# Operations charged by their measured steps, and two weight stages moved into attention

## The chip, the cores and the metric

The kernel runs on one core of one Trainium2 chip. The metric is the device time of one execution in microseconds (us), lower is better. A core has five engines with queues of their own: PE (matmul; PEld is its weight load), DVE (vector), ACT (scalar), POOL and SP, of which POOL and SP issue nearly all DMAs here. Each engine works its queue strictly in order, and engines wait for each other by semaphores.

## The reference

Three layers follow each other, all in float32. `q`, `k`, `v` are [4, 12, 448, 64]; `x` of the second layer is [1792, 768].

```python
scores = scale * np.matmul(q, k.transpose(0, 1, 3, 2)) - np.log(S)
attn = np.matmul(1.0 / (1.0 + np.exp(-scores)), v)            # sigmoid, no softmax
x = attn.transpose(0, 2, 1, 3).reshape(1792, 768)
h = np.maximum(np.maximum(x @ w1, x @ w2), x @ w3) @ moe_w_out   # weights 768 x 768
h = h @ w_in                                                  # 768 x 2048
g = np.maximum(h, 0.0) + alpha * np.minimum(h, 0.0)
out = g @ w_out                                               # 2048 x 768
```

## The kernel before

**Products.** Every matrix product after attention is a 2 x 2 block product with seven multiplications in place of eight (Strassen and Winograd): an index `k` from 0 to 6 names the multiplication, sums of blocks stand on either side. Each float32 operand is split into a high and a low word ("h" and "l"), and three matmuls (l by h, h by l, h by h) make one product of full precision. A step `(u, k, g)` is 9 matmuls of 128 x 128 by 128 x 448 for unit `u`, multiplication `k`, token half `g`; a unit has 14 steps. Units 0 to 8 are the first product (three column blocks for each of `w1`, `w2`, `w3`; the maximum is taken on DVE as units arrive), then units 100 to 105 the product with `moe_w_out` (`third` in the code, its left operands made first of all, in attention, and stored in DRAM), then units 9 to 16 the product with `w_in`; the product with the last `w_out` follows in 42 groups of 24 matmuls (`e_group`).

**Words.** The weights arrive as 64-bit floats, half a block at a time (128 x 384, tile `wr`, four buffers), and `word_ops` makes float32 of them with integer operations: two on ACT (L240, L243) and three on DVE (L250, L251, L259). With `early=True` the first of the ACT ones goes to DVE instead (L247). `unit_ops` takes four halves, makes four sums (L289), and cuts seven operands `f_0` to `f_6` into high (L278, on ACT, or on DVE for `moe_w_out`) and low word (L282, DVE). These are the left sides of a unit's steps. `words_out` makes four more halves per unit for the last product and stores them to DRAM. The pool `ws` holds words and cut operands in 21 buffers; a cut `f_k` of unit `u` may be made once step `(u-1, k, 1)` stands in the program, which frees its two buffers.

**Who sets the order.** PE's order is written out by hand. The rest is filled in by a planner: `op` puts an operation with an engine letter ("A", "D", "Q" for a DMA) and a price in columns into a list; after each step of PE `advance` gives ACT and DVE credit (`STEP`, two thirds of it for ACT) and `emit`s whatever is ready while its engine's credit is above zero. A price is the operation's columns plus 150. What PE needs and has not been emitted yet is forced out by `need`. Evictions of a step's result (ACT copies at L852 and L867, DVE sums and maxima at L289) are emitted right behind the step and charged by `spend`.

**Around the change.** In attention (12 units of 7 chunks) `load_half` brings in the first four weight halves during unit 1, the `moe_w_out` operands are planned at `(u, c) == (1, 0)`, those of unit 0 at `(4, 0)`. At the first step of unit `u`, `begin` plans the operands of unit `u + 1`. `h_store` forms sums of the finished maxima after every third unit and stores them; `held` names the ones that must be out before the next unit writes there, and `evict` forces all of them at its first eviction.

Of the kernel before, what the change touches and what calls it, by code (L numbers as in the profile page):

```python
# [62 lines left out]
def kernel(  # L63
# [11 lines left out]
    B, H, S, D = BATCH, HEADS, SEQ, P // 2  # L75
# [7 lines left out]
    HF = HK * P  # L83
# [42 lines left out]
    halves, zc, zu, zo = half_blocks()  # L126
# [13 lines left out]

    class Op:
        def __init__(self, engine, cols, fn, deps, gate, lag):
            self.engine, self.cols, self.fn, self.deps, self.gate = engine, cols + 150, fn, deps, gate
            self.step, self.ends, self.after = None, [], []

            self.lag = lag
# [1 line left out]

    free = {"wr": 8, "wl": 4, "wk": 8, "ws": 5, "wf": 4, "rr": 14, "e": 4, "a": 7}
    urgent, flow = [], []
    STEP = 1700
    credit = {"A": 0, "D": 0}

    def op(engine, cols, fn, *deps, gate=None, soon=False, lag=0):
# [41 lines left out]
                    n += 1  # L198

    def spend(engine, cols):  # L200
        credit[engine] -= cols + 150

    maker = {}

# [26 lines left out]
    def word_ops(z, gate=None, early=False):  # L231


        st = {}

        def first():
            st["r"] = wraw.pop(z)
            st["T"] = wslot(f"wt{z}", U32)
            if not early:
                nc.scalar.activation(  # L240
                    st["T"].bitcast(F32), st["r"][:, :, 1].bitcast(F32), AF.Abs, scale=2.0**-112
                )
            nc.scalar.activation(st["r"][:, :, 0], st["r"][:, :, 0], AF.Copy, scale=2.0**-29)  # L243

        def whole():
            if early:
                nc.vector.tensor_scalar(  # L247
                    st["T"].bitcast(F32), st["r"][:, :, 1].bitcast(F32), 2.0**-112, None, ALU.mult
                )
            nc.vector.tensor_scalar(st["T"], st["T"], 3, None, ALU.logical_shift_left)  # L250
            nc.vector.scalar_tensor_tensor(  # L251
                out=st["r"][:, :, 0],
                in0=st["r"][:, :, 1],
                scalar=0x80000000,
                in1=st["r"][:, :, 0],
                op0=ALU.bitwise_and,
                op1=ALU.bitwise_or,
            )
            nc.vector.tensor_tensor(out=st["T"], in0=st["r"][:, :, 0], in1=st["T"], op=ALU.add)  # L259
            word[z] = st["T"].bitcast(F32)  # L260
            if z >= 20:
                load_half(z + 4)

        o = op(
            "A", (1 if early else 2) * HF, first,
            gate=lambda: z in since and tick[0] > since[z] + 3 and (gate is None or gate()),
        )
        o = op("D", (4 if early else 3) * HF, whole, o)
        if z < 20:

            op("Q", 0, lambda: load_half(z + 4), o, lag=1)
        return o

    def split_ops(dst, make, src, w, *deps, engine="A", **kw):

        def hi():
            dst[0] = make("h")
            (nc.scalar.copy if engine == "A" else nc.vector.tensor_copy)(dst[0], src())  # L278

        def lo():  # L280
            dst[1] = make("l")
            nc.vector.tensor_sub(dst[1], src(), dst[0].bitcast(F32))  # L282

        o = op("D", w, lo, op(engine, w, hi, *deps, **kw), soon=kw.get("soon", False))
        maker[id(dst)] = o
        return o

# [4 lines left out]

    cd = {}
    pending = [0]

    def words_via(z):

# [14 lines left out]

        return back

    def unit_ops(u, z, gates=None, words=word_ops, store=False, more=[]):

        f = [{} for _ in range(7)]
        t = {}
# [20 lines left out]
        def cut(k, src, *deps):  # L339
            def make(x):  # L340
                if store and x == "h":
                    pending[0] += 1
                return wslot(f"f{u}_{k}{x}", F32R)

            o = split_ops(f[k], make, src, HF, *deps, gate=gates[k], engine="D" if store else "A")
            cuts.append(o)
            if store:
                cd[u, k] = [dpool.tile([P, HF], F32, tag=f"c{u}{k}{x}", name=f"cd{u}_{k}{x}") for x in "hl"]

                def put():  # L350
# [151 lines left out]
    def attention(apool, ps_s, ps_v):  # L502
# [118 lines left out]
        for u in range(nu):  # L621
            for c in range(NK):
                scores(u, c)
                if c == 0 and u:
                    for m in (NK - 2, NK - 1):
                        av(u - 1, m)
                    close(u - 1)
                elif c > 1:
                    av(u, c - 2)
                    if u == 0 and c in (4, 5):  # L630
                        to_x(0, 0, (5 - c,))
                if u == 1 and 1 <= c <= 4:
                    load_half(c - 1)
                if (u, c) == (1, 0):
                    for r in range(HK):
                        done += unit_ops(-1 - r, zc[r], words=lambda z: word_ops(z, early=True), store=True)
                if (u, c) == (2, 2):
                    nc.sync.dma_start(out=alpha_sb, in_=alpha)
                if (u, c) == (4, 0):
                    free_ws = lambda: all(o.step is not None for o in done)  # L640
                    unit_ops(0, zu[0], words=lambda z: word_ops(z, gate=free_ws))
                if u and c == 1:
                    load_v(u + 1, nc.gpsimd)
                if u and c < 4:
                    load(u + 1, "kq"[c % 2], c // 2)
                if c == 0:
                    advance(1800, 800)
                elif c != 1:
                    advance(1400, 450)
# [31 lines left out]
    def ff(ps_m, swap, turn_left):  # L681
# [4 lines left out]
        L = ND0 - 1  # L686
# [72 lines left out]
        def h_store(u, g):  # L759
# [14 lines left out]
                b["T"] = slot(f"h{g}{r}_t", "c")  # L774
                tensor_op(b["T"], B12, B11, ALU.subtract)

            put(0, lambda: B11)
            o21, o22 = put(1, lambda: B21), put(6, lambda: B22)
            o1 = op("D", TW, t1, soon=True)
            p1 = put(2, lambda: b["T"], o1)  # L780
            o3 = op("D", TW, lambda: tensor_op(B12, B22, B12, ALU.subtract), o1, soon=True)
            put(4, lambda: B12, o3)
            o2 = op("D", TW, lambda: tensor_op(b["T"], B22, b["T"], ALU.subtract), p1, soon=True)
            put(3, lambda: b["T"], o2)
            o4 = op("D", TW, lambda: tensor_op(B21, B21, b["T"], ALU.subtract), o2, o21, soon=True)
            held[g] = [o22, put(5, lambda: B21, o4)]

        def evict(u, g, i, t, src, other=None):

# [18 lines left out]
            j = u % 3  # L808
            key = (i, 2 * g + t)
            if j == 0:  # L810
                if g in held:
                    need_ops(*held.pop(g))
                cur[key] = slot(f"mx{u}_{i}_{key[1]}", "c")
            if other is not None:
                dst = other if j else cur[key]
# [147 lines left out]
        def begin(u):  # L963
# [2 lines left out]
            elif u == ND0:  # L966
                pass
            elif u != L:
                last[:] = unit_ops(u + 1, zu[u + 1])
                if u < NU - 3:  # L970
                    words_out(u)
                elif u < L:
# [7 lines left out]
                    for r in range(HK - 1):  # L980
                        reload(0, c, r, lambda: (L, 0, 0) in made)

        via, last = [], []
        began, run = set(), []
        inner = (0, 2, 3, 1, 4, 6, 5)
        third = [(0, 0)]
# [403 lines left out]
```

## Time and profile before

| | |
|---|---|
| device time, median of 3 runs | 928.92 us (928.04 to 932.2) |
| profiled execution, its own time | 928.69 us |
| its span, first to last instruction | 926.8 us |
| PE, DVE, ACT, POOL busy | 94%, 71%, 57%, 16% of the span |
| mean granted PE clock | 0.983 |

All durations are from the profiled execution, and places are us from the start of its span. Attention lasts to 132.9, the first product to 412.6, that with `moe_w_out` to 500.5, that with `w_in` to 719.4, the last to 923.4. PE's busy time is modelled, so that the number of its matmuls in a stretch tells more than the share.

### The profile page before, as it was taken

To read this page: it belongs to the slowest core of one execution; us is meant where nothing else is said; L and a number is where in the kernel's file an instruction comes from. 1 tells how busy PE (TensorE), PEld (TensorE's weight loads), DVE (VectorE), ACT (ScalarE), POOL (GpSimd) and SP (SyncE) were. 2 spreads that over 40 slices of the span, in tenths; PEclk is the share of its full clock that TensorE was granted. 3 is DMA by queue.
4 is the path that set the end of the run, shared out by engine and by line. 5 is a ranking of instruction groups with operands and counts; after the bars stand their busy time and mean duration, and the time that the engine had idled before them with its cause. 6 is when DMAs were issued, how large, how long until landed. Compare 5 with 4: busy or idle time off the path is not lost.

```text
span 926.8 us, 14153 instructions
## 1 busy us (share of the span) xinstructions
PE 869.6 (94%) x4878; PEld 765.1 (83%) x4878; DVE 654.3 (71%) x1289; ACT 527.8 (57%) x1021; POOL 148.5 (16%) x276
## 2 busy tenths in 40 slices
PE   9999997698889989887999899989999999999998
PEld 4478985687778878776999799978999999999997
DVE  1767766477778878765767788887876958777741
ACT  6888975345355445454546667667666735444520
POOL 2454000001300131331000013321221100000110
PEclk9999999899999999999999999999999999999999
DMA  7899510245644665688663146643445889644411
GB/s 240 286 333 340 166 54 0 70 135 149 221 145 136 183 212 170 204 302 277 205 194 103 40 154 213 232 168 129 168 168 177 304 306 392 238 144 149 151 51 50
DMA packets 77607, 170.45 MB, mean 184 GB/s; under 512 B 11120, under 2 KB 51856, under 8 KB 77536
## 3 DMA queue, kind: packets, MB, share of 16 engines
q1 hardware_dynamic: 59472, 104.81, 36.6%
q0 software_dynamic: 17776, 64.41, 18.9%
q8 instruction: 38, 0.62, 0.3%
q10 hardware_dynamic: 288, 0.34, 0.1%
q14 instruction: 33, 0.27, 0.1%
HBM read 123.12 MB, written 46.40 MB: 183 GB/s over the span
## 4 chain that ended last, share of the span: by engine, by line
PE 85%; DVE 11%; issue 2%; ACT 2%; DMA 0%; POOL 0%; DVEq 0%; ACTq 0%; POOLq 0%
PE u_0X L672 15%; PE u_1X L672 13%; PE eW L672 9%; PE eX L672 9%; PE u_0W L672 7%; PE sc L543 7%; PE pav L564 7%; PE u_1W L672 7%; PE u_0V L672 4%; PE u_1V L672 3%; PE eV L672 3%; DVE mx L289 2%; DVE wr L251 1%; DVE u L289 1%; DVE wt L259 1%
## 5 line engine op out<-in xcount | busy, mean ns | idle before, releaser
L543 PE MATMUL sc<-qt,kt 64*64 64x448 f32 x672 | 108.2, 541 | 0.1
L564 PE MATMUL pav<-a,vt 64*64 64x448 f32 x672 | 106.8, 537 | 0.0
L551 ACT ACTIVATE a<-sc,bias_s 128x896 f32<-128x896 f32 x84 | 83.3, 1008 | 15.2 <-PE sc L543 14.1
L543 PEld LDWEIGHTS sc<-qt,kt 64*64 64x64 f32 x672 | 55.7, 134 | 21.0 <-issue 12.9
L259 DVE CUSTOM_DVE_ANT_0 wt<-wr,wt 128x768 uint16<-128x768 uint16 x112 | 62.6, 559 | 3.9
L564 PEld LDWEIGHTS pav<-a,vt 64*64 64x64 f32 x672 | 54.0, 132 | 13.6 <-issue 7.8
L251 DVE SCALAR_TENSOR_TENSOR wr<-wr 128x384 uint32<-128x384 uint32 x112 | 61.9, 553 | 3.7 <-ACT wr L243 3.1
L243 ACT ACTIVATE wr<-wr 128x384 uint32<-128x384 uint32 x112 | 61.5, 550 | 1.4 <-DVE f-1_3h L278 0.7
L867 ACT COPY u<-u_0X 128x448 f32<-128x448 f32 x40 | 21.3, 534 | 66.7 <-PE u_0X L672 66.7
L240 ACT ACTIVATE wt<-wr 128x384 f32<-128x384 f32 x100 | 55.2, 552 | 0.4 <-DMA wr<-in_weights_dram 0.4
L752 POOL DMA_DIRECT2D gd<-r x48 | 26.1, 544 | 163.0 <-DVE r L719 150.9
L719 DVE SCALAR_TENSOR_TENSOR r<-n,nalpha,r 128x448 f32<-128x448 f32 x64 | 42.9, 682 | 11.3 <-ACT n L716 10.8
L938 POOL DMA_DIRECT2D wd<-wt x32 | 17.4, 544 | 197.6 <-DVE wt L259 186.8
L289 DVE TENSOR_TENSOR u<-u_0W,u 128x448 f32<-128x448 f32 x34 | 21.2, 623 | 35.7 <-ACT u L867 31.5
L289 DVE TENSOR_TENSOR u<-u_1W,u 128x448 f32<-128x448 f32 x34 | 21.2, 623 | 31.5 <-ACT u L867 20.6
L250 DVE TENSOR_SCALAR wt<-wt 128x384 uint32<-128x384 uint32 x112 | 40.1, 358 | 3.5 <-ACT wt L240 3.0
L867 ACT COPY u<-u_1X 128x448 f32<-128x448 f32 x40 | 21.4, 534 | 32.8 <-PE u_1X L672 32.8
L579 DVE COPY x<-pav 128x448 f32<-128x448 f32 x12 | 7.5, 625 | 33.7 <-PE pav L564 33.7
L672 PE MATMUL u_0W<-x_2h,f_2l 128*128 128x448 f32 x27 | 12.2, 453 | 19.6 <-DVE f_2l L282 19.6
L852 ACT COPY u_0V<-u_0X 128x448 f32<-128x448 f32 x20 | 10.3, 517 | 31.8 <-PE u_0X L672 31.8
L1264 ACT COPY p<-eW 128x448 f32<-128x448 f32 x12 | 6.4, 533 | 32.9 <-PE eW L672 32.9
L672 PEld LDWEIGHTS u_0W<-x_2h,f_2l 128*128 128x128 f32 x27 | 5.9, 217 | 23.0 <-DVE f_2l L282 22.6
(814 smaller groups left out, 2832.4 us busy)
## 6 DMA issues: line engine op xcount, KB each, us to landing
wr<-in_weights_dram SPq DMA_DIRECT2D x96, 384.0 KB, 3.5
gl<-gd SPq DMA_DIRECT2D x79, 224.0 KB, 4.3
wl<-wd SPq DMA_DIRECT2D x64, 192.0 KB, 4.5
gd<-r POOLq DMA_DIRECT2D x48, 224.0 KB, 2.8
gl_T<-gdT SPq DMA_DIRECT2D x32, 224.0 KB, 5.1
hr<-hd POOLq DMA_DIRECT2D x28, 224.0 KB, 5.3
wr<-in_weights_dram POOLq DMA_DIRECT2D x16, 384.0 KB, 6.0
wd<-wt POOLq DMA_DIRECT2D x32, 192.0 KB, 3.8
```

Of the source, the lines that this page charges most:

```text
L240: nc.scalar.activation(st["T"].bitcast(F32), st["r"][:, :, 1].bitcast(F32), AF.Abs, scale=2.0**-112)
L243: nc.scalar.activation(st["r"][:, :, 0], st["r"][:, :, 0], AF.Copy, scale=2.0**-29)
L250: nc.vector.tensor_scalar(st["T"], st["T"], 3, None, ALU.logical_shift_left)
L251: nc.vector.scalar_tensor_tensor(out=st["r"][:, :, 0], in0=st["r"][:, :, 1], scalar=0x80000000, in1=st["r"][:, :, 0], op0=ALU.bitwise_and, ...
L259: nc.vector.tensor_tensor(out=st["T"], in0=st["r"][:, :, 0], in1=st["T"], op=ALU.add)
L289: nc.vector.tensor_tensor(out=out, in0=a, in1=b, op=op)
L543: nc.tensor.matmul(sc[g * KH : (g + 1) * KH, j, :S], keys[u, z][r, m * KH : (m + 1) * KH], queries[u, z][r], start=True, stop=True,)
L551: nc.scalar.activation(a, sc[:, :, :S], AF.Sigmoid, bias=bias_s, scale=scale)
L564: nc.tensor.matmul(pv[key][j * D : (j + 1) * D, :S], vts[u][r, m, j], a[r, j], start=start, stop=stop,)
L672: nc.tensor.matmul(ps[:, : rh.shape[-1]], lt, rh, start=(start and z == 0), stop=(stop and z == len(mms) - 1), skip_group_check=True,)
L719: nc.vector.scalar_tensor_tensor(out=s["r"], in0=s["n"], scalar=nalpha[:, f : f + 1], in1=s["r"], op0=ALU.mult, op1=ALU.add,)
L867: nc.scalar.copy(side[u, g, k], banks[X][:, :TW])
```

## The change

Prices come closer to the distance at which operations follow each other: 100 columns on top for ACT and 90 for DVE in place of 150, a high word cut on DVE at half its columns, 100 more for the whole-word operation, and `STEP` is 1760 in place of 1700. The first weight halves are loaded during attention's unit 0, the `moe_w_out` operands are planned at `(0, 4)` in place of `(1, 0)`. Unit 0's words are made the early way and its high words cut on DVE. Unit 1 is planned at attention's unit 9; so `begin` of unit 0 plans nothing, and each later `begin` the next unit as before. `held` becomes four lists, forced one at each of the four evictions.

```diff
+    EXTRA = {"A": 100, "D": 90, "L": 0, "Q": 0}
-            self.engine, self.cols, ... = engine, cols + 150, ...
+            self.engine, self.cols, ... = engine, cols + EXTRA[engine], ...
-    STEP = 1700
+    STEP = 1760
-        o = op("D", (4 if early else 3) * HF, whole, o)
+        o = op("D", (4 if early else 3) * HF + 100, whole, o)
-        o = op("D", w, lo, op(engine, w, hi, *deps, **kw), soon=kw.get("soon", False))
+        o = op("D", w, lo, op(engine, w if engine == "A" else w // 2, hi, *deps, **kw), soon=...)
-    def unit_ops(u, z, gates=None, words=word_ops, store=False, more=[]):
+    def unit_ops(u, z, gates=None, words=word_ops, store=False, engine="A"):
-            o = split_ops(f[k], make, src, HF, *deps, gate=gates[k], engine="D" if store else "A")
+            o = split_ops(f[k], make, src, HF, *deps, gate=gates[k], engine=engine)
...
-                if u == 1 and 1 <= c <= 4:
-                    load_half(c - 1)
-                if (u, c) == (1, 0):
+                if u == 0 and c > 2:
+                    load_half(c - 3)
+                if (u, c) == (0, 4):
                     for r in range(HK):
-                        done += unit_ops(-1 - r, zc[r], words=lambda z: word_ops(z, early=True), store=True)
+                        done += unit_ops(..., words=lambda z: word_ops(z, early=True), store=True, engine="D")
...
-                    unit_ops(0, zu[0], words=lambda z: word_ops(z, gate=free_ws))
+                    unit_ops(0, zu[0], words=lambda z: word_ops(z, gate=free_ws, early=True), engine="D")
+                if (u, c) == (9, 0):
+                    last[:] = unit_ops(1, zu[1], words=lambda z: word_ops(z, early=True))
...
-            held[g] = [o22, put(5, lambda: B21, o4)]
+            held[g] = [[p0], [p4], [o22, o2, o3], [p3, put(5, lambda: B21, o4)]]
-                if g in held:
-                    need_ops(*held.pop(g))
+                if held.get(g):
+                    need_ops(*held[g].pop(0))
...
-                last[:] = unit_ops(u + 1, zu[u + 1])
+                if u:
+                    last[:] = unit_ops(u + 1, zu[u + 1])
```

PE's order is the same in both kernels, instruction by instruction. DVE's changes throughout. Before, around the low word `f6_2l`, which unit 6 needs at its fifth step (`u5` and `mx` are evictions, `h01_t` and `h11_t` sums of `h_store`, `wt` words):

```order
L251 SCALAR_TENSOR_TENSOR wr58_3184<-wr58_3184 128x384
L259 ISA wt58_3259<-wr58_3184,wt58_3259 128x768
L289 TENSOR_TENSOR mx3_0_3_2774<-mx3_1_3_2696,mx3_0_3_2774 128x448
L289 TENSOR_TENSOR h01_t_3297<-mx3_1_1_2679,h01_t_3297 128x448
L289 TENSOR_TENSOR mx3_1_0_2717<-mx3_1_0_2717,h01_t_3297 128x448
L250 TENSOR_SCALAR wt59_3277<-wt59_3277 128x384
L251 SCALAR_TENSOR_TENSOR wr59_3207<-wr59_3207 128x384
L259 ISA wt59_3277<-wr59_3207,wt59_3277 128x768
L289 TENSOR_TENSOR h11_t_3342<-mx3_1_3_2696,h11_t_3342 128x448
L289 TENSOR_TENSOR mx3_1_2_2735<-mx3_1_2_2735,h11_t_3342 128x448
L289 TENSOR_TENSOR wu6_3412<-wt58_3259,wt59_3277 128x384
L282 TENSOR_TENSOR f6_2l_3416<-wu6_3412,f6_2h_3414 128x384
L289 TENSOR_TENSOR wt58_3259<-wt56_3186,wt58_3259 128x384
```
It stands behind unit 5's last maximum (`mx3_0_3`, from step `(5, 6, 1)`) and behind the sums of `h_store`. After, the same operation:

```order
L252 TENSOR_SCALAR wt60_3228<-wt60_3228 128x384
L253 SCALAR_TENSOR_TENSOR wr60_3155<-wr60_3155 128x384
L261 ISA wt60_3228<-wr60_3155,wt60_3228 128x768
L284 TENSOR_TENSOR f6_2l_3267<-wu6_3226,f6_2h_3245 128x384
L291 TENSOR_TENSOR wt56_3134<-wu6_3226,wt56_3134 128x384
L252 TENSOR_SCALAR wt61_3231<-wt61_3231 128x384
L253 SCALAR_TENSOR_TENSOR wr61_3160<-wr61_3160 128x384
L261 ISA wt61_3231<-wr61_3160,wt61_3231 128x768
L291 TENSOR_TENSOR u5_0_4_3286<-u5_0W_3199,u5_0_4_3286 128x448
L291 TENSOR_TENSOR mx3_1_1_2765<-u5_0_4_3286,mx3_1_1_2765 128x448
L291 TENSOR_TENSOR wt57_3137<-wt57_3137,wt56_3134 128x384
```
It now stands ahead of `u5_0_4`, the eviction of step `(5, 4, 0)`, ten steps of PE before the step that reads it.

DVE at the start of the `moe_w_out` product, before (`h0_00l` and its like are the low words of the reloaded maxima, read by that product's first steps; `u8_1_4` is evicted after step `(8, 4, 1)`, the step before):

```order
L282 TENSOR_TENSOR h0_1l_4135<-mx6_1_0_3542,h0_1h_4118 128x448
L289 TENSOR_TENSOR mx6_0_1_3581<-mx6_1_1_3502,mx6_0_1_3581 128x448
L289 TENSOR_TENSOR u8_1_4_4151<-u8_1W_3991,u8_1_4_4151 128x448
L289 TENSOR_TENSOR mx6_1_3_3524<-u8_1_4_4151,mx6_1_3_3524 128x448
L282 TENSOR_TENSOR h0_00l_4159<-hr0_00_3898,h0_00h_3987 128x448
L282 TENSOR_TENSOR h0_01l_4161<-hr0_01_3900,h0_01h_3989 128x448
L282 TENSOR_TENSOR h0_2l_4175<-h0_t_4120,h0_2h_4137 128x448
```
After, where `u8_0_4` is the eviction of step `(8, 4, 0)` and `u7_1_3` belongs to the unit before:

```order
L291 TENSOR_TENSOR u7_1_3_3829<-u7_1W_3780,u7_1_3_3829 128x448
L291 TENSOR_TENSOR mx6_0_3_3676<-u7_1_3_3829,mx6_0_3_3676 128x448
L284 TENSOR_TENSOR f8_5l_3935<-wt75_3746,f8_5h_3904 128x384
L284 TENSOR_TENSOR f8_6l_3951<-wt73_3701,f8_6h_3937 128x384
L284 TENSOR_TENSOR h0_00l_4050<-hr0_00_3965,h0_00h_4030 128x448
L284 TENSOR_TENSOR h0_01l_4052<-hr0_01_3967,h0_01h_4032 128x448
L284 TENSOR_TENSOR h0_20l_4054<-hr0_20_3969,h0_20h_4034 128x448
L291 TENSOR_TENSOR mx6_0_0_3456<-u8_0V_3949,mx6_0_0_3456 128x448
L284 TENSOR_TENSOR h0_21l_4074<-hr0_21_3971,h0_21h_4056 128x448
L284 TENSOR_TENSOR h0_30l_4076<-hr0_30_3989,h0_30h_4058 128x448
L284 TENSOR_TENSOR h0_31l_4078<-hr0_31_3991,h0_31h_4060 128x448
L291 TENSOR_TENSOR u8_0_4_4093<-u8_0W_4001,u8_0_4_4093 128x448
```
The low words for multiplications 0, 2 and 3 moved ahead of unit 8's middle.

POOL's queue at the start, before (`vt` are value blocks for attention, `wr` weight halves; `vt2` waits for a buffer that unit 0 frees):

```order
L532 DMA vt0_99<-in_v_dram 64x512
L532 DMA vt1_116<-in_v_dram 128x896
L137 DMA wr0_268<-in_weights_dram 128x768
L532 DMA vt2_270<-in_v_dram 128x896
L137 DMA wr1_287<-in_weights_dram 128x768
L137 DMA wr2_304<-in_weights_dram 128x768
L137 DMA wr3_321<-in_weights_dram 128x768
```
After:

```order
L535 DMA vt0_99<-in_v_dram 64x512
L535 DMA vt1_116<-in_v_dram 128x896
L137 DMA wr0_156<-in_weights_dram 128x768
L137 DMA wr1_172<-in_weights_dram 128x768
L137 DMA wr2_229<-in_weights_dram 128x768
L137 DMA wr3_243<-in_weights_dram 128x768
L535 DMA vt2_282<-in_v_dram 128x896
```
The halves `wr1` to `wr3` moved ahead of `vt2` and its wait.

## Rows read from the trace of the kernel before

**Rows 1.** The page: busy time of engines; the chain that ended last, by engine.

```profile
PE 869.6 (94%) x4878; PEld 765.1 (83%) x4878; DVE 654.3 (71%) x1289; ACT 527.8 (57%) x1021; POOL 148.5 (16%) x276
...
PE 85%; DVE 11%; issue 2%; ACT 2%; DMA 0%; POOL 0%; DVEq 0%; ACTq 0%; POOLq 0%
```

**Rows 2.** Waits of PE: us in total, times, longest us; 3 of 19 rows.

```profile
PE u_0W L672 <- DVE f_2l L282: 25.3, 11, 3.3
...
PE u_0X L672 <- DVE h_00l L282: 2.3, 1, 2.3
...
PE u_1X L672 <- DVE x_0l L282: 0.2, 1, 0.2
```

**Rows 3.** By stage: us; PE, PEld, DVE, ACT, POOL busy (instructions); PEclk, DMA, GB/s.

```profile
0.00:132.90 132.90, 131.54 (x1350) 95.37 (x1350) 81.87 (x177) 110.05 (x145) 40.64 (x77) 1.00 0.73 247
132.90:412.60 279.70, 243.09 (x1118) 216.22 (x1117) 201.38 (x409) 135.61 (x285) 41.73 (x78) 0.96 0.51 154
412.60:500.50 87.90, 79.90 (x380) 71.43 (x379) 58.39 (x108) 42.86 (x87) 5.86 (x11) 0.98 0.67 215
500.50:719.40 218.90, 211.15 (x1029) 193.29 (x1028) 174.60 (x339) 148.85 (x321) 44.94 (x83) 0.99 0.47 158
719.40:923.40 204.00, 203.97 (x1009) 188.75 (x1007) 137.67 (x257) 90.10 (x183) 15.33 (x29) 1.00 0.58 200
```

**Rows 4.** The chain, whole span, final stage: start us, us, what.

```profile
719.52 29.12 PE eX L672 x144
```

**Rows 5.** The chain between units 2 and 3 of the first product.

```profile
236.62 0.64 DVE u L289
...
247.06 0.57 DVE f_2l L282
...
247.68 3.65 PE u_0W L672 x9
...
253.14 1.82 PE u_0X L672 x9
```

**Rows 6.** DVE at the same place, in order: start us, us, what.

```profile
240.21 0.55 DVE L282 TENSOR_TENSOR f_1l<-wt,f_1h 128x384 fp32r<-128x384 f32 x1
240.68 0.35 DVE L250 TENSOR_SCALAR wt<-wt 128x384 uint32<-128x384 uint32 x1
240.95 0.55 DVE L251 SCALAR_TENSOR_TENSOR wr<-wr 128x384 uint32<-128x384 uint32 x1
241.53 0.56 DVE L259 CUSTOM_DVE_ANT_0 wt<-wr,wt 128x768 uint16<-128x768 uint16 x1
242.01 0.62 DVE L289 TENSOR_TENSOR h_t<-mx,h_t 128x448 f32<-128x448 f32 x1
```

**Rows 7.** Groups on DVE, whole span: busy us, mean ns of one.

```profile
L259 DVE CUSTOM_DVE_ANT_0 wt<-wr,wt 128x768 uint16<-128x768 uint16 x112 | 62.6, 559 | 3.9
L251 DVE SCALAR_TENSOR_TENSOR wr<-wr 128x384 uint32<-128x384 uint32 x112 | 61.9, 553 | 3.7 <-ACT wr L243 3.1
L250 DVE TENSOR_SCALAR wt<-wt 128x384 uint32<-128x384 uint32 x112 | 40.1, 358 | 3.5 <-ACT wt L240 3.0
L282 DVE TENSOR_TENSOR f_2l<-wu,f_2h 128x384 fp32r<-128x384 f32 x17 | 9.4, 552 | 1.8 <-ACT f_2h L278 1.7
L289 DVE TENSOR_TENSOR mx<-u,mx 128x448 f32<-128x448 f32 x24 | 15.0, 625 | 0.8
L247 DVE TENSOR_SCALAR wt<-wr 128x384 f32<-128x384 f32 x12 | 4.3, 355 | 0.0
```

**Rows 8.** Two units of attention; columns as in Rows 3.

```profile
78.00:88.50 10.50, 10.50 (x117) 8.90 (x113) 8.19 (x19) 9.01 (x12) 5.36 (x10) 1.00 1.00 376
120.20:130.70 10.50, 10.50 (x117) 9.53 (x113) 5.84 (x11) 9.82 (x15) 0.00 (x0) 1.00 0.03 10
```

**Rows 9.** Waits in attention, the weight loads of PE on key loads.

```profile
PEld sc L543 <- DMA kt<-in_k_dram: 1.3, 2, 0.8
```

**Rows 10.** In the `w_in` product, units 11 and 12; columns as in Rows 3.

```profile
580.00:600.00 20.00, 20.00 (x101) 18.54 (x100) 17.89 (x36) 13.32 (x30) 7.12 (x13) 1.00 0.61 210
```

More of the change, by code (lines that the diff above doesn't have):

```diff
@@ L138, in load_half @@
         wraw[z], since[z] = t, tick[0]
+    EXTRA = {"A": 100, "D": 90, "L": 0, "Q": 0}
     class Op:
         def __init__(self, engine, cols, fn, deps, gate, lag):
-            self.engine, self.cols, self.fn, self.deps, self.gate = engine, cols + 150, fn, deps, gate
+            self.engine, self.cols, self.fn, self.deps, self.gate = engine, cols + EXTRA[engine], fn, deps, gate
             self.step, self.ends, self.after = None, [], []
@@ L200, in spend @@
     def spend(engine, cols):
-        credit[engine] -= cols + 150
+        credit[engine] -= cols + EXTRA[engine]
     maker = {}
@@ L282, in lo @@
             nc.vector.tensor_sub(dst[1], src(), dst[0].bitcast(F32))
-        o = op("D", w, lo, op(engine, w, hi, *deps, **kw), soon=kw.get("soon", False))
+        o = op("D", w, lo, op(engine, w if engine == "A" else w // 2, hi, *deps, **kw), soon=kw.get("soon", False))
         maker[id(dst)] = o
@@ L294 @@
     pending = [0]
+    last = []
     def words_via(z):
@@ L631, in attention @@
                         to_x(0, 0, (5 - c,))
-                if u == 1 and 1 <= c <= 4:
-                    load_half(c - 1)
-                if (u, c) == (1, 0):
+                if u == 0 and c > 2:
+                    load_half(c - 3)
+                if (u, c) == (0, 4):
                     for r in range(HK):
-                        done += unit_ops(-1 - r, zc[r], words=lambda z: word_ops(z, early=True), store=True)
+                        done += unit_ops(-1 - r, zc[r], words=lambda z: word_ops(z, early=True), store=True, engine="D")
                 if (u, c) == (2, 2):
@@ L775, in t1 @@
                 tensor_op(b["T"], B12, B11, ALU.subtract)
-            put(0, lambda: B11)
+            p0 = put(0, lambda: B11)
             o21, o22 = put(1, lambda: B21), put(6, lambda: B22)
@@ L781, in h_store @@
             o3 = op("D", TW, lambda: tensor_op(B12, B22, B12, ALU.subtract), o1, soon=True)
-            put(4, lambda: B12, o3)
+            p4 = put(4, lambda: B12, o3)
             o2 = op("D", TW, lambda: tensor_op(b["T"], B22, b["T"], ALU.subtract), p1, soon=True)
-            put(3, lambda: b["T"], o2)
+            p3 = put(3, lambda: b["T"], o2)
             o4 = op("D", TW, lambda: tensor_op(B21, B21, b["T"], ALU.subtract), o2, o21, soon=True)
-            held[g] = [o22, put(5, lambda: B21, o4)]
+            held[g] = [[p0], [p4], [o22, o2, o3], [p3, put(5, lambda: B21, o4)]]
         def evict(u, g, i, t, src, other=None):
@@ L981, in begin @@
                         reload(0, c, r, lambda: (L, 0, 0) in made)
-        via, last = [], []
+        via = []
         began, run = set(), []
```

## The prediction

> **What bounds the kernel now.** I read the chain of waits first, then the stages, then PE's waits, then the chain at one place. By the chain PE carries 85% and DVE 11% [rows 1]: the reader is to see that little else matters, and that the 11% lie where PE stands.
>
> How much does PE lose, and where? In the last product 144 matmuls take 29.12 us back to back, 0.2022 us each [rows 4], so a step of 9 is 1.82 us. Matmuls of the stages behind attention: 4878 in all less 1350 up to 132.9 [rows 1, 3], so 3528, or 3528 x 0.2022 = 713.4 us. They took 923.4 - 132.9 = 790.5 us. **77.1 us are lost.** By stage, length less count x 0.2022 (a matmul over a border counts twice, so these fall a little short): first product 279.7 - 1118 x 0.2022 = 53.6, `moe_w_out` 87.9 - 380 x 0.2022 = 11.1, `w_in` 218.9 - 1029 x 0.2022 = 10.8, last 0 [rows 3].
>
> On what does it wait? Of 19 waits of PE 18 lie behind attention, 52.0 us together. 46.6 of them are for low words `f_k` and `h` made on DVE (`f_2l` alone 25.3 in 11 times) [rows 2], the other 5.4 for x, y and a copy, down to 0.2. The rest of the 77.1 comes after the waits: the granted clock is 0.96 in the first product, 0.98 and 0.99 in the next two and 1.00 where PE never stands [rows 3]. Half clock (1.2 GHz) for a part p makes the mean 1 - p/2, so the matmul time not granted is at most 0.04 x 279.7 + 0.02 x 87.9 + 0.01 x 218.9 = 15 us; in the chain the first nine matmuls after a stall take 3.65 us and later ones 1.82 [rows 5]. The remaining 10 are short restarts.
>
> Why are the low words late? Between units 2 and 3 the chain leaves PE at 236.6 and runs through DVE to `f_2l` at 247.06, and PE goes on at 247.68 [rows 5]; DVE's operations follow each other there without a gap [rows 6]. The low word is the last of a queue, and the order shows what stands ahead of it: the previous unit's evictions, the `h_store` sums, words of later blocks. The planner gets a unit's operands out only when PE already asks for them.
>
> **The change, part by part.**
>
> *Lead.* Unit 1's four halves and two of its sums leave the first product: 4 x (0.553 + 0.559 + 0.358) for words and 2 x 0.55 for sums (of `f_2l`'s shape) = 7.0 us of DVE [rows 7]. From then on each `begin` plans one unit further ahead than PE needs, since unit 0's has nothing to plan. In the two orders `f6_2l` moves from behind unit 5's last maximum to ahead of the eviction of step (5, 4, 0), ten steps or 18.2 us ahead of the step that reads it; call that its lead. Counted in the same way, the lead of `f_2l` rises from 0 or 1 to 9 or more in all of units 2 to 8, that of the reloaded `h` of the first half from 0 or 1 to 7 or more (the last block's least is 2), and the shortest of units 10 to 15 in `w_in` from 0 to 3. In the trace every wait for an `f` or `h` has a lead of 0 or 1 in the order of before; nothing with 2 or more is waited for. So all of the 46.6 us go, and what they left behind with them.
>
> *Can DVE carry it without the stops?* One unit of the first product costs DVE 4 halves x 1.47 + 7 low words x 0.55 + 4 sums x 0.55 for the operands (11.9), 5.9 for four halves of `words_out`, and for evictions 4, 12 or 20 operations of 0.62 (mean 7.5) [rows 7]: 25.3 us against 14 x 1.82 = 25.5 of PE. By durations that is full. But operations overlap: `f_1l` lasts 0.55 and the next starts after 0.47, L250 0.35 and 0.27, L259 0.56 and 0.48; only L251 keeps its successor away for 0.58 [rows 6]. By these distances a half costs 1.33, a low word or sum 0.47, an eviction 0.54: 16 less, 10.5 + 5.3 + 6.4 = 22.2 us, 87%. I take the distances, because units 11 and 12 show it running: DVE busy 17.89 of 20.00 and PE 20.00 of 20.00, clock 1.00 [rows 10]. The Trainium skill, "Perfetto Trace Analysis", section "Per-engine timelines", says that a DVE slice in a profile lasts until its last write is acknowledged, while the next may begin its prefetch when execution ends; by that rule the sum is 22.2, by slices added up 25.3, and the distances in the trace agree with the rule.
>
> A late eviction does no harm at once: of 8 PSUM banks a unit takes 6, and the earliest reuse lies five steps (9.1 us) behind an eviction.
>
> *Clock and restarts.* They follow the stalls; where a stall goes its half clock goes. The price of both together is 77.1 - 52.0 = 25.1 us; with 46.6 of the waits gone I count them gone in full, and cover that by the residue.
>
> *What is late next.* x, y and the copy: 5.4 us of waits at most; the y of the last block move from a lead of 0 to 2 or 3 steps, unit 0's x from 0 to 3. Bounds 0 and 5.4 plus as much again for clock and restarts, 10.8; I take 3.5, nearer the low end since every lead rises.
>
> *Attention.* It gains work: unit 0 on DVE 4 x 0.355 (L247) + 7 high words, which I bound by L247's 0.355 and the 0.55 of a low word and take at 0.355, so 3.9; unit 1 4 x 1.83 + 2 x 0.55 = 8.4; and 17 sums and low words of x, which stood behind attention in the order and stand inside it now, x 0.62 = 10.5. DVE rises from 81.9 to 104.7 of 132.9 [rows 3, 7]. ACT loses 11 operations of unit 0 and gains 18 (4 of unit 1, 14 high words of x): at 0.55, as for a low word, 3.9 on top of 110.0 [rows 3]. What hides it is PE: a unit of attention is 10.5 us of PE in 10.5, while DVE has 8.2 and ACT 9.0 to 9.8 [rows 8]. If that cover goes, ACT's sigmoids are late and PE waits with them. The weight loads come earlier (`wr1` to `wr3` no longer stand behind `vt2`), and the `moe_w_out` operands and their stores closer together, while the DMA engines are already at a share of 1.00 and 376 GB/s around 80 us [rows 8]. Bounds: -1.3 (the only wait there for key loads, which could vanish [rows 9]) and +12 (the 12.3 of new weight work in full on the path). I take +1.0, near the rows that show PE untouched at the same DMA share. By the Trainium skill, "Perfetto Trace Analysis", section "Roofline", one core is bounded by its 16 DMA engines at about 435 GB/s, which would leave 59 of room over the 376; the row's share of 1.00 leaves none. By the Trainium skill's figure attention costs 0, by the row some of the 12.
>
> *Prices, `held`, `STEP`.* They are what sets the order, counted above; forcing four short lists costs nothing that is not in the eviction sums.
>
> **Sum.** 926.8 - 77.1 + 3.5 + 1.0 = 854.2 span; the execution was 1.9 longer than its span (928.69), so 856.1; the median of the three runs is 0.2 above that execution: **856.3 us**.
>
> **The rivals.**
>
> *DVE becomes the bound of the first product.* For it: 25.3 of 25.5 by durations, and units 2 and 5 with 20 evictions reach 11.9 + 5.9 + 12.4 = 30.2, 4.7 too much each, unit 8 nearly so; DVE also stands behind copies of ACT. Against it: rows 10, and a lead of ten steps that absorbs 4.7. Time: three units x (4.7 + 1.8 for a step at half clock, 3.65 - 1.82 in rows 5) = 19.5, so 876.
>
> *Attention grows.* DMA at its limit delays keys, values or the release of `ws` buffers, and DVE's copies out of PSUM come late. For it: share 1.00. Against: PE 10.50 of 10.50 at that share, one key wait of 1.3. Time: half to all of the 12 on the path in place of 1.0, 861 to 867.
>
> *Slower than before: the `ws` buffers run out.* 21 buffers; unit 0 holds 14 cut operands when attention ends, unit 1's words and sum 5, which leaves 2. If in-order ACT and DVE then sit in front of buffers that PE frees only at the end of a unit, a unit's operands fall behind the previous unit's last step instead of beside it: 10.5 us of DVE at each of 8 borders, 84 us against the 53.6 lost now in the first product. 928.7 + 30 = 959. It decides from 6.7 us a border. Against it: a cut is planned only once the step that frees its two buffers stands ahead of it, and the order shows the cuts running ten steps ahead.
>
> **How the numbers follow.** Forecast (850.5 to 861): 0.70. Attention grows (861 to 867): 0.12. DVE bound (868 to 884): 0.13. Buffers (959): 0.03. Something that keeps the lead from becoming time, near 929: 0.02. The low end is all of 77.1 and the 1.3 gone: 928.9 - 78.4 = 850.5. The high end reaches into the DVE rival, 872, which leaves out less than 2 in 10. Half a per cent, 4.6 us, is about what a measurement of this kernel tells from no change; only the last two cases come near it or pass it: faster 0.95, same 0.02, slower 0.03.
>
> **What would show it.** Right: PE's waits for `f_2l` under 2 us in total; the first product some 228 us long, its granted clock 1.00, DVE above 80% busy in it (201.4 less 7.0 and 10.5, over 228); attention's end within 2 us of 132.9 with DVE about 80% busy; the `w_in` stage near 209. Wrong: attention past 135, PE waiting for keys or pav for DVE's copies; first-product stalls that stay with DVE gapless in front of them (the DVE rival), or with ACT or DVE idle and released by PE (the buffers).

## The result and the profile after

The changed kernel takes **855.15 us** (median of four runs, 854.7 to 855.51) against 928.78 us (four runs of the kernel before, one more than in its table); the ratio is 0.920, with a 95% interval of 0.9177 to 0.9224. The forecast was 856.3. The profiled execution has a span of 853.2 us and a granted clock of 1.00 from end to end.

The page of the changed kernel, busy time and the chain that ended last:

```profile
PE 846.6 (99%) x4878; PEld 735.2 (86%) x4878; DVE 654.6 (77%) x1304; ACT 516.5 (61%) x1006; POOL 149.0 (17%) x276
...
PE 96%; DVE 2%; DMA 1%; ACT 0%; issue 0%; ACTq 0%
```

DVE is busy for as long as before, 654.6 us against 654.3, and its 11% of the chain [rows 1] have become 2%. No work went away; it was put where PE doesn't wait for it. The stages of the changed kernel, columns as in the rows by stage of before:

```profile
0.00:133.90 133.90, 132.60 (x1350) 73.56 (x1350) 100.86 (x223) 112.56 (x152) 40.55 (x77) 1.00 0.74 257
133.90:361.80 227.90, 226.05 (x1118) 209.34 (x1117) 190.42 (x389) 125.55 (x269) 44.96 (x82) 1.00 0.62 190
361.80:438.20 76.40, 76.40 (x379) 70.87 (x379) 54.13 (x100) 40.82 (x84) 3.26 (x6) 1.00 0.69 221
438.20:645.70 207.50, 207.50 (x1028) 192.49 (x1027) 172.61 (x336) 147.98 (x319) 44.80 (x83) 1.00 0.49 163
645.70:849.80 204.10, 204.04 (x1009) 188.92 (x1008) 136.20 (x257) 89.27 (x185) 15.41 (x29) 1.00 0.59 204
```

Against [rows 3] attention is 1.0 longer, the first product 51.8 shorter, `moe_w_out` 11.5, `w_in` 11.4, the last 0.1 longer: 73.6 us net, as between the spans. These are all of PE's waits after; none is for a low word any more [rows 2]:

```profile
PE u_0X L677 <- ACT u L872: 1.8, 1, 1.8
PE warm L612 <- DVE zeros L608: 1.2, 1, 1.2
```

I use one more measure below, the **loss**: the time from one step's first matmul to the next one's, less 1.820 us, summed over the steps behind attention up to the last product. It was 76.8 us before and is 2.2 now.

What is left of it is one place. ACT there (start us, us, line, operation; in brackets how long it stood and what ended that):

```profile
171.57 0.54 ACT L245 ACTIVATE wr<-wr 128x384 uint32<-128x384 uint32 x1
175.07 0.51 ACT L280 CAST f_2h<-wu 128x384 fp32r<-128x384 f32 x1 [2.96 <-DMA wd<-wt]
175.49 0.53 ACT L872 COPY u<-u_0X 128x448 f32<-128x448 f32 x1
```

And the chain through it (start us, us, what):

```profile
171.22 3.77 DMA wd<-wt
...
175.07 0.51 ACT f_2h L280
175.59 0.44 ACT u L872
...
176.07 2.09 PE u_0X L677 x9
```

The high word `f_2h`, some twelve steps early, takes a `ws` buffer whose last content is still being stored by `words_out`. ACT works in order, so the copy `u`, which PE needs now, stands behind a cast that nobody needs yet.

### The profile page after: what moved, and what is told of

It reads as the page before. It is cut to its first block, busy times and chain, and to the rows that moved or that the text cites. A ratio compares the mean times of both kernels' runs of the same rounds, so it can differ in the third digit from the quotient of the medians.

```text
span 853.2 us, 14217 instructions
## 1 busy us (share of the span) xinstructions
PE 846.6 (99%) x4878; PEld 735.2 (86%) x4878; DVE 654.6 (77%) x1304; ACT 516.5 (61%) x1006; POOL 149.0 (17%) x276
## 4 chain that ended last, share of the span: by engine, by line
PE 96%; DVE 2%; DMA 1%; ACT 0%; issue 0%; ACTq 0%
PE u_0X L677 17%; PE u_1X L677 17%; PE eW L677 10%; PE eX L677 10%; PE u_0W L677 8%; PE u_1W L677 8%; PE sc L546 7%; PE pav L567 7%; PE u_0V L677 4%; PE u_1V L677 4%; PE eV L677 3%; DMA wr<-in_weights_dram 1%; DMA wd<-wt 0%; PE warm L612 0%; DVE wr L253 0%
## 5 line engine op out<-in xcount | busy, mean ns | idle before, releaser
L546 PE MATMUL sc<-qt,kt 64*64 64x448 f32 x672 | 91.7, 539 | 0.0
L554 ACT ACTIVATE a<-sc,bias_s 128x896 f32<-128x896 f32 x84 | 82.7, 1008 | 12.0 <-PE sc L546 11.3
L567 PE MATMUL pav<-a,vt 64*64 64x448 f32 x672 | 89.8, 538 | 0.0
L546 PEld LDWEIGHTS sc<-qt,kt 64*64 64x64 f32 x672 | 40.5, 134 | 29.9 <-issue 15.7
L567 PEld LDWEIGHTS pav<-a,vt 64*64 64x64 f32 x672 | 38.6, 133 | 27.4 <-issue 13.1
L242 ACT ACTIVATE wt<-wr 128x384 f32<-128x384 f32 x92 | 51.0, 554 | 13.9 <-DMA wr<-in_weights_dram 10.5
L720 ACT ACTIVATE r<-u 128x448 f32<-128x448 f32 x32 | 18.6, 580 | 6.8 <-DVE u L291 6.8
L291 DVE TENSOR_TENSOR p<-eX,p 128x448 f32<-128x448 f32 x12 | 7.5, 621 | 16.4 <-PE eX L677 16.4
```

Source lines behind the costliest of these rows:

```text
L242: nc.scalar.activation(st["T"].bitcast(F32), st["r"][:, :, 1].bitcast(F32), AF.Abs, scale=2.0**-112)
L291: nc.vector.tensor_tensor(out=out, in0=a, in1=b, op=op)
L546: nc.tensor.matmul(sc[g * KH : (g + 1) * KH, j, :S], keys[u, z][r, m * KH : (m + 1) * KH], queries[u, z][r], start=True, stop=True,)
L554: nc.scalar.activation(a, sc[:, :, :S], AF.Sigmoid, bias=bias_s, scale=scale)
L567: nc.tensor.matmul(pv[key][j * D : (j + 1) * D, :S], vts[u][r, m, j], a[r, j], start=start, stop=stop,)
```

## Experiments

The first four ask which part of the change brings the gain. Theory A: the lead in the written order decides, wherever it comes from. Theory B is the prediction's own wording: unit 1, planned in attention, puts every later unit one ahead. The leads below were counted in each kernel's order; they are exact, and only the times had to be measured. A lead is the number of steps from the one behind which the low word was emitted to the one that reads it, and 0 where `need` forced it out right ahead of its reader. (The prediction counted the ten steps of `f6_2l` from the next step on; by the table's count it is 11.)

| kernel | charge / credit | f_2, f_3 lead, unit 2 | unit 5 | unit 8 | least h | f_0, f_2, unit 13 | loss, us | median, us |
|---|---|---|---|---|---|---|---|---|
| before | 99% | 0, 0 | 1, 0 | 0, 0 | 0 | 2, 0 | 76.8 | 928.78 |
| changed | 91% | 12, 12 | 11, 11 | 9, 8 | 2 | 8, 4 | 2.2 | 855.15 |
| prices only | 91% | 8, 7 | 10, 10 | 9, 8 | 2 | 8, 4 | 2.2 | 855.86 |
| moves only | 99% | 9, 6 | 8, 7 | 7, 3 | 2 | 2, 0 | 20.6 | 874.72 |
| changed, unit 1 late | 91% | 11, 10 | 11, 11 | 9, 8 | 2 | 8, 4 | 0.4 | 854.06 |
| unit 1's move alone | 99% | 0, 0 | 0, 0 | 0, 0 | 0 | 2, 0 | 115.9 | 967.12 |
| before, STEP 1820 | 93% | 2, 1 | 4, 4 | 6, 5 | 2 | 8, 4 | 20.4 | 872.37 |
| prices only, STEP 1560 | 103% | 3, 2 | 1, 1 | 0, 0 | 0 | 2, 0 | 54.0 | 905.95 |

"Charge / credit" is what three units of the first product charge to DVE in the planner, once it runs evenly, against the credit of their 42 steps: before, 54,252 columns of planned operations (units 3 to 5) and 28 evictions of 598, 70,996 of 71,400; with the new prices 67,218 of 73,920.

**Prices only.** The kernel before with this and no move (in short form):

```diff
-    cols + 150                                       # all engines
+    cols + {"A": 100, "D": 90}                       # ACT, DVE
-    STEP = 1700
+    STEP = 1760
-    op("D", (4 if early else 3) * HF, whole, o)
+    op("D", (4 if early else 3) * HF + 100, whole, o)
-    op(engine, w, hi, ...)
+    op(engine, w if engine == "A" else w // 2, hi, ...)
```

> The kernel before with the new prices and STEP alone; no work is moved into attention and `held` stays. Theory A (what counts is the lead in the written order, wherever it comes from): by the order the least lead of an f in units 1 to 8 is 3, and that of the first half's reloaded h is 2, nearly as in the changed kernel; so f and h waits under 3 us, first product 228 to 231 us at clock 1.00, attention's end at 132.9, total 855 to 860. Theory B (the prediction's own words: unit 1 planned in attention is what puts each unit one ahead): without that move most of the stalls stay, total 895 to 929.

Measured 855.86 us (853.8 to 858.61), ratio 0.9206 (0.917 to 0.9243), which can't be told from the whole change. Its stages, attention and the first product:

```profile
0.00:136.00 136.00, 130.59 (x1350) 55.79 (x1350) 86.88 (x185) 112.12 (x152) 40.76 (x77) 1.00 0.72 242
136.00:364.00 228.00, 227.01 (x1121) 208.94 (x1118) 200.55 (x412) 133.47 (x284) 44.57 (x82) 1.00 0.62 197
```

The first product takes 228.0 us with 200.6 us of DVE in it, as much DVE as before had in 279.7. So not a microsecond of DVE work had to leave that stage, and the old form of `held` costs nothing measurable either. Theory A holds, B falls. That attention ends at 136.0 here, 3.1 later than expected, is taken up below.

**Moves only** (the changed kernel with the four old numbers):

> The changed kernel with the old prices (150 for all, STEP 1700, high word at full price); all moves and `held` kept. Theory A: leads of f in units 1 to 8 are 3 to 12 in the order, so the first product is 228 to 231 us; but in units 10, 13 and 14 of the w_in stage the leads are 0 and 1 as before, so that stage stays at 217 to 219 us; total 864 to 868. If the prices were what makes the whole gain: above 900. If the moves were: 855 to 857.

Measured 874.72 us (871.48 to 877.32); above the range that A gave. PE's waits there:

```profile
PE u_0W L677 <- DVE f_2l L284: 6.2, 3, 3.0
PE u_0X L677 <- DVE f_0l L284: 2.6, 1, 2.6
PE u_1X L677 <- DVE x_5l L284: 1.4, 1, 1.4
```

The `w_in` stage stalls as expected where the lead is 0 or 1 (14.1 us of loss in units 9, 10, 13 and 14; 11.3 before). What I had left out are the x words of unit 0, 6.5 us, whose leads I hadn't counted for this kernel (the four that are waited for have 0, 0, 0 and 1). From unit 1 to the end of `moe_w_out` nothing is lost: the moves give a head start, and at 99% charge the planner loses it only slowly. So the moves together also bring most of the gain; which of them gives the head start is not shown.

**Unit 1 late** (the changed kernel without the move that the prediction rested on):

```diff
-                if (u, c) == (9, 0):
-                    last[:] = unit_ops(1, zu[1], words=lambda z: word_ops(z, early=True))
-                if u:
-                    last[:] = unit_ops(u + 1, zu[u + 1])
+                last[:] = unit_ops(u + 1, zu[u + 1], ...)     # unit 1's words still early
```

> The changed kernel, but unit 1 is planned at the first step of unit 0 again (its words still made the early way, on the DVE). Theory A: in the order the leads of unit 1's f are 4 to 9 and those of all later units as in the changed kernel, so 853 to 857, although 7 us of DVE work return to the first product. Theory B (that move is what gives the lead): 895 to 929.

Measured 854.06 us (852.5 to 855.18): as fast as the changed kernel, by theory A. The 7 us of DVE that went back cost no time, and the 1.85 us stall was not there.

**Unit 1's move alone** (the same lines added to the kernel before):

> The kernel before, with nothing but unit 1 planned in attention's unit 9. Theory A: in the order f_2 and f_3 of units 1 to 8 and the first half's h still have a lead of 0, so the stalls stay: 915 to 930. Theory B: 860 to 880.

Measured **967.12 us** (961.81 to 968.08), ratio 1.039 (1.0346 to 1.0433): slower than before, which neither theory had. PE's first three waits:

```profile
PE u_0W L675 <- DVE f_2l L282: 27.9, 11, 3.5
PE u_0X L675 <- DVE f_0l L282: 16.5, 8, 3.2
PE u_0V L675 <- DVE f_1l L282: 10.9, 6, 2.5
```

Now `f_0l` and `f_1l` are waited for as well. Attention, columns as in the rows by stage:

```profile
0.00:131.80 131.80, 130.57 (x1350) 79.55 (x1350) 81.92 (x177) 109.90 (x145) 40.73 (x77) 1.00 0.74 249
```

DVE does the same 177 operations there as before [rows 3]: unit 1 was planned in attention, but none of its work was done there. Its operations only stood in the planner's list ahead of x's. So this run shows what the earlier place in the list does, and not what 7 us less of DVE in the first product would do. DVE in front of unit 2's `f_0l`:

```profile
206.02 0.56 DVE L259 CUSTOM_DVE_ANT_0 wt<-wr,wt 128x768 uint16<-128x768 uint16 x1
206.50 0.62 DVE L289 TENSOR_TENSOR u<-u_0W,u 128x448 f32<-128x448 f32 x1
207.15 0.62 DVE L289 TENSOR_TENSOR mx<-u,mx 128x448 f32<-128x448 f32 x1
207.76 0.62 DVE L289 TENSOR_TENSOR u<-u_1W,u 128x448 f32<-128x448 f32 x1
208.42 0.62 DVE L289 TENSOR_TENSOR mx<-u,mx 128x448 f32<-128x448 f32 x1
208.96 0.55 DVE L282 TENSOR_TENSOR f_0l<-wt,f_0h 128x384 fp32r<-128x384 f32 x1
```

It is made behind the previous unit's last evictions, and by the order the `f_0` of units 2 to 8 all have a lead of 0 or 1. Unit 0 lost 21.0 us instead of 14.5, and each later unit of the first product some 8.3 (before 5.0). I read this as a backlog that unit 0 leaves and that is never worked off. That made a new theory C: what decides is the charge of a unit against the credit of its 14 steps. Credit that isn't used doesn't add up (`advance` caps it), so by this theory a backlog stays at a charge of 99%, whatever made it, and is worked off where the charge is well below its credit.

**One number in the kernel before**, `STEP = 1820`:

> The kernel before with one number changed, STEP 1820 in place of 1700. Theory C (new, from the first four runs: what decides is the sum of prices of a unit against the credit of its 14 steps): in units 3 to 5 of the kernel before DVE is charged 70,996 columns of 71,400 of credit, 99%, so a backlog is never worked off; here it is 93%, and in the order the leads grow from 0 and 1 in unit 1 to 4 and more from unit 4 on, and no f of the w_in stage falls under 3. So stalls in units 0 and 1 only (10 to 20 us of the 77), 862 to 874. If it is the single prices or the moved work that counts, it stays above 900.

Measured 872.37 us (870.61 to 872.91), inside the range of C. Two stretches, the 28 steps of units 0 and 1 (51.0 us at full pace, so 16.8 lost) and what follows, where the clock is back at 1.00:

```profile
131.40:199.20 67.80, 56.35 (x257) 49.57 (x254) 44.98 (x90) 34.58 (x74) 2.21 (x4) 0.95 0.25 72
199.20:380.00 180.80, 178.62 (x878) 163.89 (x877) 161.84 (x334) 104.61 (x220) 42.17 (x78) 1.00 0.70 225
```

The loss is 11.1 us in unit 0, 5.8 in unit 1, 1.2 in unit 2 and 2.3 in all the rest, `moe_w_out` and `w_in` included (0.0 each). One number undoes nearly three quarters of the 76.8 us.

**The new prices, too little credit**, `STEP = 1560`:

> The first experiment (new prices, no moves) with STEP 1560 in place of 1760, so that DVE is charged 67,218 of 65,520 columns in units 3 to 5, 103%. Theory C: the leads in the order shrink again, f_2 and f_3 from 3 in units 1 and 2 to 1 in units 3 to 5 and 0 in units 6 to 8, the first half's h 0, units 10, 13 and 14 as in the kernel before: stalls of some 15 us in units 6 to 8, 11 in the moe_w_out stage, 11 in w_in, a few at a lead of 1: 890 to 902. If the single prices are what counts, 855 to 860.

Measured 905.95 us (902.7 to 907.93), 4 above the range and 50 above the same prices at 1760. The loss by units is 2.4, 1.5, 1.5 in units 3 to 5, then 6.8, 6.3, 6.3, and 14.7 in `moe_w_out`: 19.4 in units 6 to 8 where I had said 15, and 14.7 where I had said 11. The lead drains away and the stalls come back as it does. A lead of 1 costs 1.5 to 2.4 us a unit. C holds in both directions.

`STEP` raises ACT's credit too, and no run was timed with one engine's credit alone. The order tells them apart. With 1820 for DVE alone, `f_2` and `f_3` have leads of 2 and 1 in unit 2, 4 and 4 in unit 5, 6 and 5 in unit 8, as in the run with both, and the least `h` has 2. With 1820 for ACT alone they have 1 and 1, 1 and 0, 0 and 0, and the least `h` 0. So up to `moe_w_out` it is DVE's charge that decides. In `w_in` it takes both: `f_2` of unit 13 keeps a lead of 0 with either alone.

**Has DVE room, and how much?** Low words of units 1 to 8 are computed again, not charged, so that the order stays. First four of them twice:

```diff
-            nc.vector.tensor_sub(dst[1], src(), dst[0].bitcast(F32))
+            for _ in range(1 + (1 if again else 0)):     # again=1 <= u <= 8 and k in (0, 1, 2, 3)
+                nc.vector.tensor_sub(dst[1], src(), dst[0].bitcast(F32))
```

> The changed kernel, in which the low words of f_0 to f_3 of units 1 to 8 are computed twice, uncharged, so that the order stays: 4 more DVE operations per unit. By start distances (0.47 each) DVE goes from 22.6 to 24.5 us in a unit of 25.5 and nothing stalls: 854 to 857. By durations added up (25.3 + 4 x 0.55 = 27.5 a unit) it is 2.0 over in each of 8 units, 16 us less the lead of about 9: 862 to 872.

Measured 854.81 us (852.98 to 855.24). Six whole units of the first product, the changed kernel's row first:

```profile
187.00:340.00 153.00, 153.00 (x759) 141.91 (x758) 135.66 (x282) 84.93 (x182) 28.42 (x52) 1.00 0.64 191
```

and with the four more:

```profile
187.00:340.00 153.00, 153.00 (x758) 141.85 (x757) 147.21 (x304) 84.22 (x182) 27.81 (x51) 1.00 0.63 191
```

DVE goes from 22.6 to 24.5 us a unit of 25.5, and PE doesn't stand for a moment in these units. By durations added up this could not be. Then all seven three times:

> The changed kernel, in which all seven low words of units 1 to 8 are computed three times, uncharged: 14 more DVE operations per unit. By distances 22.6 + 14 x 0.47 = 29.2 against 25.5: 3.7 over in each of six full units, 22 us, of which the lead absorbs 9 to 18, and each stall brings some half clock: 859 to 872. By durations added up 25.3 + 7.7 = 33.0, 7.5 over, 45 to 60 us less the same lead: 882 to 906.

Measured 893.46 us (891.88 to 894.75), outside the range by distances; the one by durations holds it, but not by its reason. The same stretch, and two of DVE's low words:

```profile
187.00:340.00 153.00, 133.59 (x623) 119.51 (x622) 148.41 (x300) 68.37 (x149) 25.02 (x46) 0.97 0.54 163
```

```profile
261.36 1.73 DVE L285 TENSOR_TENSOR f_0l<-wt,f_0h 128x384 fp32r<-128x384 f32 x3
263.01 1.74 DVE L285 TENSOR_TENSOR f_1l<-wt,f_1h 128x384 fp32r<-128x384 f32 x3
264.67 0.35 DVE L252 TENSOR_SCALAR wt<-wt 128x384 uint32<-128x384 uint32 x1
```

Two things were off. Three of them keep the next one away for 1.65, not 3 x 0.47: an operation that writes the same tile as the one before it follows at (1.65 - 0.47) / 2 = 0.59. So 14 more cost 8.3 us, and a unit 22.6 + 8.3 = 30.9; measured are 31.3 (unit 3 starts at 216.1 and unit 8 at 372.7, five units later). And the lead absorbed next to nothing, because it isn't the low words that come late. PE's waits:

```profile
PE u_0X L678 <- ACT u L873: 16.1, 10, 3.0
PE u_1X L678 <- ACT u L873: 9.1, 5, 2.3
```

ACT, which is 45% busy there, stands in front of casts that wait for DVE's sums, with the copies PE needs behind them:

```profile
263.71 0.51 ACT L873 COPY u<-u_0X 128x448 f32<-128x448 f32 x1
266.71 0.51 ACT L280 CAST f_2h<-wu 128x384 fp32r<-128x384 f32 x1 [2.48 <-DVE wu L292]
267.13 0.55 ACT L242 ACTIVATE wt<-wr 128x384 f32<-128x384 f32 x1
267.58 0.54 ACT L245 ACTIVATE wr<-wr 128x384 uint32<-128x384 uint32 x1
268.02 0.52 ACT L873 COPY u<-u_1X 128x448 f32<-128x448 f32 x1
```

So when DVE is the bound, a table of PE's waits names ACT.

**Attention, and a better version.** The last four ran side by side on one chip. The changed kernel again:

> The changed kernel, unaltered, for a second profile and as the yardstick of the next three. If attention's 1.0 us belongs to the change, its end lies at 133.5 to 134.3 again; if it is where transfers happen to land, it may lie anywhere from 131.8 to 136, as in the profiles so far. Total 854 to 856.

Measured 856.16 us (854.93 to 857.23), ratio 0.9202 (0.9179 to 0.9225). Its first product starts at 135.41, not 133.91: 2.5 us behind [rows 3], with the same instructions. In the two runs that repeat low words, whose attention has the changed kernel's operations in the same order on DVE, ACT and POOL, it starts at 134.58 and 132.24. So one order ends anywhere within 3.2 us, over at least two chips, and a difference below that says nothing from one profile. With the first loads and the `moe_w_out` operands as late as before:

> The changed kernel, but the first four weight halves are loaded in attention's unit 1 and the moe_w_out operands planned at (1, 0), as in the kernel before; unit 1 stays in attention. If the early loads cost attention its 1.0 us, units 1 and 2 are 10.52 long again, attention ends at 132 to 133, and the total is 853 to 854.5; if the early planning is needed, the weights come late behind attention and it is above 857.

Measured 855.66 us (853.96 to 855.92). That is above the 853 to 854.5 of the first theory and below the 857 of the second. Units 1 and 2 are 10.52 us long again, but units 4 and 5 take 11.95 and 11.56 in their place, and attention ends at 134.0. Unit 2 is 10.52 long in the two runs that repeat low words, too, with the loads early. So no effect of the early loads on attention's end is shown. Last, two places mended:

```diff
-            gate=lambda: z in since and tick[0] > since[z] + 3 and (...)
+            gate=lambda: z in since and tick[0] > since[z] + (6 if early else 3) and (...)
-            o = split_ops(f[k], make, src, HF, *deps, gate=gates[k], engine=engine)
+            o = split_ops(f[k], make, src, HF, *deps, gate=gates[k], engine=engine, lag=2 if u == 2 else 0)
```

> The changed kernel with the two late places mended: a half that is made the early way is taken up 6 ticks after its load is issued instead of 3, so that ACT doesn't stand before a transfer in attention's units 1 to 4; and the high words of unit 2 are cut two steps later, so that ACT doesn't stand before the store wd<-wt at 175. Attention ends at 131.8 to 133.3 and the 1.85 us stall goes: 852 to 854.

Measured **852.01 us** (850.94 to 852.7), ratio 0.9156 (0.9134 to 0.9179): 0.5% under the changed kernel on that chip, 852.7 at most against 854.9 at least. Behind attention the loss is 0.05 us. The first product and `moe_w_out`:

```profile
133.80:361.60 227.80, 227.80 (x1129) 211.15 (x1128) 193.08 (x394) 127.28 (x273) 44.90 (x82) 1.00 0.61 193
361.60:438.00 76.40, 76.40 (x379) 70.84 (x378) 53.35 (x100) 40.86 (x84) 3.27 (x6) 1.00 0.65 213
```

Of the 3.7 us between the two profiled spans (854.6 and 850.9) 2.0 are the stall at 175 and 1.6 attention, which ends at 133.77, later than the 133.3 expected. Those 1.6 lie within the 3.2 of one order, so that the six ticks shorten attention is not shown. Which of the two edits takes the stall away is not shown: both move what stands ahead of it in ACT's queue, and `f_2h` there runs at 170.98 without a wait.

> The third experiment (unit 1 planned at the first step of unit 0) with the same 6 ticks: nothing is lost behind attention, and attention ends at 132 to 134 instead of 135.8: 851.5 to 854.

Measured 852.78 us (852.13 to 853.48), ratio 0.9166 (0.9144 to 0.9188); attention ends at 133.6, and 0.6 us are lost behind it. With unit 1 made in the first product, as in the kernel before, it can't be told from the best.

## Why the prediction was right, and where it was not

**The loss, and that it would go.** 77.1 us were counted lost, 2.2 are left. That PE waits for an `f` or `h` only at a lead of 0 or 1 held in the four experiments that have such waits, with one exception of 0.5 us at a lead of 2 (`f_2` of unit 2 with `STEP` 1820).

**What makes the lead: wrong.** The prediction's step was: "From then on each `begin` plans one unit further ahead than PE needs, since unit 0's has nothing to plan." The code alone contradicts it: `begin` of unit `u` plans unit `u + 1` in both kernels, and only unit 1 is planned earlier. The leads were read rightly from the order, but this isn't where they come from. Without that move they are the same from unit 3 on, with 10 or more in unit 2 (854.06), and the move alone, which put none of unit 1's work into attention, makes the kernel slower (967.12). That the forecast held all the same is because it took the leads from the written order, not from this reason. What is enough by itself is the part to which the prediction gave one sentence, "they are what sets the order, counted above": the prices (855.86). The moves together bring much at the old prices too (874.72), so they are not without effect, but with the new prices they add nothing that was measured. A low word was charged 534 columns of 1700 to a step of 1.82 us, 0.57 us, and takes 0.47 [rows 6]; now it is charged 474 of 1760, 0.49. With the old prices a unit's charge came to 99% of its credit, and the planner believed in a DVE that was full, though DVE was busy for 201.4 of 279.7 us. The 7.0 us that leave the first product were worth nothing in time, since DVE had the room.

**DVE's room.** Forecast 22.2 us a unit by start distances, measured 22.6 (135.66 over six units); the durations' 25.3 is refuted by the run with four more. The 0.54 taken for an eviction is too short for some: where the next operation reads its result, that one starts 0.65 later (206.50 to 207.15 in the rows of unit 1's move alone). By the Trainium skill ("Perfetto Trace Analysis", section "Per-engine timelines") a DVE slice lasts until its last write is acknowledged, while the next operation may begin its prefetch when execution ends; slices of 0.55 at distances of 0.47 agree with that. In the whole stage DVE is busy 83.6% of 227.9; above 80 was forecast.

**Clock and restarts.** 25.1 us were counted to go with the stalls, and the clock is 1.00 throughout.

**Residue.** Forecast 3.5, measured 2.2, and of another kind: not x, y or a copy that DVE makes late, but ACT held by a store. This is the rival of the `ws` buffers in small, released by a DMA rather than by PE, at one border of eight and for 1.85 us, where the rival had 10.5 at each.

**Attention.** Forecast +1.0, measured 0.97 in the first profile and 2.5 in the second, so the agreement is chance. The kernel with `STEP` 1820 and the one with unit 1's move alone have before's order of attention to its end and start the first product at 131.39 and 131.83, before at 132.94; the four profiles of the changed order lie between 132.24 and 135.41, and the one with the prices alone, which has a third order, is at 136.0. A difference of 1 us there is within what one order shows; that attention grew somewhat is likely from these ends, but how much is open. What a late unit looks like is seen in unit 2, where a sigmoid of ACT stands behind a weight load:

```profile
25.54 7.14 DMA wr<-in_weights_dram
...
32.76 0.04 ACT wr L245
...
33.23 1.01 ACT a L554
```

The DMA engines are at their limit around it:

```profile
30.00:40.00 10.00, 9.95 (x104) 4.19 (x100) 7.56 (x20) 7.80 (x12) 6.24 (x11) 1.00 1.02 388
```

By the Trainium skill's 435 GB/s or so ("Perfetto Trace Analysis", section "Roofline") there would be room of 47 over these 388; the share of 1.02 has none, and transfers of 7.1 us go with the share. DVE was forecast at 104.7 us in attention and is at 100.9: there the prediction had added durations.

**Rivals.** DVE as the bound begins between 24.5 and 30.9 us a unit, and the change is at 22.6. PE's weight loads wait for keys for 1.3 us in attention, as before [rows 9], and the time that attention's growth would have cost, 861 and up, didn't come.

**Sum.** 854.2 us of span were forecast, 853.2 measured: 1.3 less residue, and 0.3 the other way, since the loss before was 76.8 and not 77.1.

## What to carry to other kernels

A planner's prices are a model of the engines, and when their sum comes near its credit, it makes an order for a machine that is slower than the real one: check charge against credit first; here one number was worth nearly three quarters of the loss. Price an operation by the distance to its successor's start, not by its duration. Before crediting a gain to the part of a change that looks like the cause, ask of the order what each part does alone; work that was planned earlier, but not done earlier, only made what stood behind it late here.

## What was not expected of the hardware

DVE's low word (128 x 384) is followed after 0.47 us by an operation on another tile and after 0.59 by one that writes the same tile, though its duration reads 0.55 in both cases. An engine that sets the pace need not be the one waited for: in the run with 14 more, DVE is busy 148.4 of 153.0 us, yet of PE's 28.0 us of waits in the first product only 2.8 are for DVE. And the end of attention differs by 1.5 us between two profiled executions of one program, and by 3.2 over four executions whose attention has the same order.
